# First attention of a transformer block: a third score buffer, values of two key tiles in one run, and the query projection over the whole array in blocks of seven passes

## The chip, the cores and the metric

The kernel runs on one core of one Trainium2 chip. A core has a matrix engine (TensorE, with a stationary operand that is loaded ahead of each multiplication), a vector engine (VectorE), an engine for functions such as exp (ScalarE), a general one (GpSimd), one that mainly issues transfers (SyncE), a working memory of 128 partitions (SBUF) and eight banks of accumulators that TensorE writes (PSUM, a bank holds 128 x 512 numbers of 4 bytes). The metric is the device time of one launch in microseconds (us), the median of several.

## The reference

One transformer block in float32: x is 2048 x 576, 32 heads of 18 numbers share one key head and one value head, and the second half is a feed-forward layer of two gates without a nonlinearity, 576 to 4608 and back.

```python
def A(x, wq, wk, wv, wo):
    q = (x @ wq).reshape(B, S, H, Dh) ...          # H = 32, Dh = 18
    k, v = x @ wk, x @ wv                          # one head for all
    p = softmax(einsum("bhqd,bkd->bhqk", q, k) * Dh ** -0.5)
    o = einsum("bhqk,bkd->bhqd", p, v)
    return o... @ wo
h = x + A(layernorm(x), ...)
n = layernorm(h)
out = h + ((n @ w_gate) * (n @ w_up)) @ w_down
```

## The kernel before, in words

The 2048 query rows are handled in four blocks of 512 (b = 0 to 3). Attention goes by groups of four heads (g = 0 to 7) and key tiles of 128 rows (t = 0 to 15); a tile has two *pairs* of heads (pr = 0 or 1), so a group has 32 pairs and a block 256. One pair is: two score matmuls (L701, 56 rows of the array each, one in the upper and one in the lower half, so that both run together) into a tile of two PSUM banks, and one exp on ScalarE over its 128 x 1024 numbers (L702), which writes a tile P in SBUF. The names are s{b}_{g}_{t}_{pr} and P{b}_{g}_{t}_{pr}. Two of the 56 rows carry an upper bound of the scores, which stands in for the maximum of the softmax.

*Values* of one key tile (L706) are four pairs of heads' products with V into four column groups of the accumulator `acc`: a run of eight matmuls in the records, in another tiling of the array (128 rows by 32 columns) than the scores (64 rows by 128 columns). `flush(n)` issues the values of the n oldest waiting tiles, in one piece. After the last tile of a group, VectorE transposes the accumulator (L732) and other steps (`run_aux`) normalise it.

Block 0 is the *first attention*. While its pairs run, the same code issues further work between them:

- `queries(b)`: the query projection of 512 rows by 126 columns (seven heads) per tile, 14 tiles in this stage. The product of two float32 matrices is made of 14 passes with a high and a low part of each side. Before, each pass is two matmuls, the upper and the lower 64 rows of the array, into two banks psq and psr (L498), which VectorE adds (L505 to L508); the result is stored to memory and fetched as the q of a group, together with the bounds.
- `bounds(b)`: sums of absolute values tq of the queries by head (L554, tile psg), split in a high and a low part by VectorE (L96, L97) and stored to `m_dram` by SyncE (L533). psg{b}_{n} begins at head n.
- `down_weights`: w_down is read, combined on GpSimd, split (L1500 on VectorE) and stored, one step for every two pairs.

The order on each engine is the order of the code (`manual_schedule`): nothing is rearranged. In `run` a loop issues pair, passes of the projection up to a budget (RATE = 2.3 of them per two pairs), pair, one auxiliary step, the values of all waiting tiles but the youngest. After the last tile of the projection (pair 208) the pools of the stage are closed and later ones are opened in the same memory, among them a second set of P tiles (P2, used in turn with the first six). After pair 226 stands the `guard`, a branch that is not taken with these inputs: it would compute exact maxima if the bound were too loose. All waiting values are issued ahead of it. Eight more pairs follow, then the other attentions mixed with the feed-forward layer, in all of which TensorE has work at every time.

PSUM before: two score tiles of two banks (tag s), two banks f, one bank m, one bank a. The accumulators of block 0 alternate between a and m up to group 5, the bound takes the one that is free:

```python
self.in_m = b == 0 and g < 6 and g % 2 == 1
return (self.ps_m if self.in_m else self.ps_a)(f"acc{b}_{g}")
```

The functions that the change touches, as they are before, with the line numbers of the profile:

## Time and profile before

| | |
|---|---|
| median of 3 runs | 2265.41 us (2263.82 to 2266.45) |
| the profiled execution | 2262.34 us, span from first to last instruction 2260.6 us |
| mean granted TensorE clock | 1.00 |
| up to pair 0 / pairs 0 to 226 / from the guard on | 43.6 / 253.9 / 1962.5 us |
| TensorE busy in the three | 31.6 / 250.7 / 1947.6 us |
| ScalarE busy in the three | 30.6 / 220.2 / 1175.8 us |
| values and scores in pairs 0 to 234 (L706, L701) | 124.4 us in 928 records, 106.1 us in 468 |
| half passes of the projection (L498) | 61.6 us in 196 records (psr) and 61.5 us in 196 (psq) |

Busy time is the union of an engine's instructions; matmuls are pipelined, so that the interval from one start to the next says more than the length of one. In rows of the timeline stand: start, length, engine, line, operation, tile written and tiles read, the part of the array that is used (rows * columns) or shapes, the count of instructions in the row, and in brackets the idle time before it on that engine and what ended it. In rows of groups "x" is the count, then come busy time, mean length in ns, and idle time before with its releaser. "PEld" is the loading of stationary operands.

### The profile page before, as it was taken

How to read it: one execution, taken by the hardware profiler on the slowest of the kernel's cores; microseconds unless marked ns; L12 is line 12 of the kernel's file. 1: busy time of each engine (PE TensorE's matmuls, PEld its weight loads, DVE VectorE, ACT ScalarE, POOL GpSimd, SP SyncE). 2: the span in 40 equal slices, each digit the busy share in tenths (PEclk: the TensorE clock that was granted, in tenths of full speed). 3: DMA queues.
4: the chain of work that ended last, by engine and by line, in shares of the span. 5: the costliest groups of instructions: out<-in, count | busy, mean ns of one | idle time of the engine just before them, and what ended most of it. 6: DMA issues, size and time to landing. Idle time of an engine off the chain costs nothing.

```text
span 2260.6 us, 45951 instructions
## 1 busy us (share of the span) xinstructions
PE 2229.9 (99%) x17972; PEld 1653.0 (73%) x17972; DVE 1381.2 (61%) x2234; ACT 1426.6 (63%) x1925; POOL 882.5 (39%) x956
## 2 busy tenths in 40 slices
PE   7999999999999999999999999999999999999999
PEld 5333345777778777777877777777777788999999
DVE  8565635555556557455555556555554667788776
ACT  7888877666666666666665666665666423555553
POOL 4445401444444444244444444433332344322222
PEclk9999999999999999999999999999999999999999
DMA  5879843555555555555455554654342435677775
GB/s 175 266 251 301 287 152 83 175 170 163 155 173 164 163 186 156 173 170 172 153 167 162 178 166 152 181 191 147 124 125 93 152 136 190 211 241 237 235 249 177
DMA packets 200433, 407.01 MB, mean 180 GB/s; under 512 B 22637, under 2 KB 54509, under 8 KB 200213
## 3 DMA queue, kind: packets, MB, share of 16 engines
q1 hardware_dynamic: 197621, 393.42, 54.4%
q0 software_dynamic: 2592, 10.62, 1.5%
q8 instruction: 143, 2.34, 0.4%
q14 instruction: 77, 0.63, 0.1%
HBM read 317.27 MB, written 74.55 MB: 173 GB/s over the span
## 4 chain that ended last, share of the span: by engine, by line
PE 81%; DMA 2%; POOL 1%; DVE 1%; ACT 1%; issue 1%; SPq 0%; ACTq 0%; POOLq 0%; DVEq 0%
PE pg L1073 17%; PE acc L706 15%; PE y L1023 12%; PE s L701 8%; PE gs L1297 8%; PE pu L1073 8%; PE yq L1262 4%; PE gu L1073 3%; PE yo L864 3%; PE gs L1304 2%; POOL h L1034 1%; PE y L993 1%; DMA out_dram<-h 1%; DMA wr<-in_wgu_dram 1%; DMA h<-in_x_dram 0%
## 5 line engine op out<-in xcount | busy, mean ns | idle before, releaser
L702 ACT ACTIVATE P<-s 128x1024 f32<-128x1024 f32 x1024 | 1009.8, 1028 | 218.8 <-PE s L701 138.3
L1073 PE MATMUL pg<-X,ws 64*128 64x512 f32 x2511 | 680.6, 389 | 0.9 <-DVE ob L719 0.9
L1073 PE MATMUL pu<-X,ws 64*128 64x512 f32 x2511 | 680.5, 389 | 0.2
L1073 PEld LDWEIGHTS pg<-X,ws 64*128 64x128 f32 x2511 | 465.0, 185 | 52.1 <-issue 2.7
L1073 PEld LDWEIGHTS pu<-X,ws 64*128 64x128 f32 x2511 | 464.2, 185 | 22.3 <-ACT tmp L1000 0.9
L706 PE MATMUL acc<-P,V 128*32 128x512 f32 x4096 | 479.9, 597 | 0.1
L701 PE MATMUL s<-q,kT 56*128 56x512 f32 x2048 | 431.4, 414 | 5.6 <-ACT P L702 4.5
L1034 POOL TENSOR_TENSOR h<-h,tmp 128x288 f32<-128x288 f32 x306 | 244.5, 829 | 335.8 <-ACT tmp L1033 333.5
L1033 ACT COPY tmp<-y 128x288 f32<-128x288 f32 x306 | 122.3, 400 | 356.0 <-PE y L1023 314.0
L701 PEld LDWEIGHTS s<-q,kT 56*128 56x128 f32 x2048 | 205.5, 184 | 166.8 <-ACT P L702 118.1
L1023 PEld LDWEIGHTS y<-wdo,room 128*128 128x128 f32 x2142 | 290.5, 188 | 47.3 <-issue 38.5
L1023 PE MATMUL y<-wdo,room 128*128 128x288 f32 x2142 | 306.8, 301 | 3.5 <-ACT tmp L1033 2.2
L706 PEld LDWEIGHTS acc<-P,V 128*32 128x32 f32 x4096 | 114.6, 109 | 254.9 <-issue 250.1
L951 DVE TENSOR_TENSOR ws<-wr,ws 128x1152 fp32r<-128x1152 f32 x108 | 189.9, 1759 | 100.0 <-POOL ws L948 100.0
L1029 DVE TENSOR_TENSOR h<-h,y 128x288 f32<-128x288 f32 x408 | 175.3, 452 | 118.0 <-PE y L1023 117.9
L1111 DVE TENSOR_TENSOR hf<-pu,hf 128x512 f32<-128x512 f32 x93 | 63.7, 685 | 223.7 <-ACT hf L1107 223.7
L948 POOL CAST ws<-wr 128x1152 fp32r<-128x1152 f32 x108 | 131.2, 1215 | 153.1 <-DMA wr<-in_wgu_dram 141.5
L96 POOL CAST room<-hf 128x256 fp32r<-128x256 f32 (+1 forms) x92 | 58.5, 636 | 319.9 <-DVE hf L1111 319.9
L1245 POOL TENSOR_TENSOR wsum<-wsum,wsum 128x512 f32<-128x512 f32 x72 | 145.2, 2017 | 45.4 <-DMA wsum<-in_wgs_dram 36.1
L97 DVE TENSOR_TENSOR room<-hf,room 128x256 fp32r<-128x256 f32 (+1 forms) x108 | 94.8, 878 | 3.3 <-ACT room L96 1.9
L1073 PE MATMUL gu<-X,ws 64*128 64x512 f32 x810 | 94.5, 389 | 0.0
L1073 PEld LDWEIGHTS gu<-X,ws 64*128 64x128 f32 x810 | 80.3, 184 | 11.9 <-issue 1.5
(268 smaller groups left out, 2759.1 us busy)
## 6 DMA issues: line engine op xcount, KB each, us to landing
wdo<-wd_dram SPq DMA_DIRECT2D x492, 288.0 KB
wr<-in_wgu_dram SPq DMA_DIRECT2D x108, 576.0 KB
wsum<-in_wgs_dram SPq DMA_DIRECT2D x108, 256.0 KB
wd_dram<-wd_room SPq DMA_DIRECT2D x20, 1008.0 KB
wsum_dram<-wsum SPq DMA_DIRECT2D x72, 256.0 KB
raw<-wsum_dram SPq DMA_DIRECT2D x72, 256.0 KB
q<-q_dram SPq DMA_DIRECT2D x64, 216.0 KB
raw<-in_wgs_dram SPq DMA_DIRECT2D x54, 256.0 KB
```

Of the source, the lines that this page charges most:

```text
L701: self.pe.matmul(s_[:, i], self.kT[o:o + 56, t * P:(t + 1) * P], q[o:o + 56, pr], start=True, stop=True)
L702: self.act.activation(p_, s_, AF.Exp, scale=SCALE)
L706: self.pe.matmul(acc[32 * j:32 * j + 32, :], self.V[:, t, :], Ps[j // 2][:, j % 2, :], start=first, stop=last, skip_group_check=True)
L948: self.nc.gpsimd.tensor_copy(w[:, 0], self.wr[n])
L951: self.dve.tensor_tensor(w[:, 1], self.wr.pop(n), f32(w[:, 0]), ALU.subtract)
L1023: pe.matmul(y[:, :HD], m[:, t * P:(t + 1) * P], k, start=(first and j == 0), stop=(j == 2), skip_group_check=True)
L1029: dve.tensor_tensor(hs, hs, y[:, :HD], ALU.add)
L1033: act.copy(z, y[:, :HD])
L1034: pool.tensor_tensor(hs, hs, z, ALU.add)
L1073: pe.matmul(ps, w[o:o + 64, wk, c], X[o:o + 64, xk, c], start=(j == 0), stop=(j == 26))
L1245: pool.tensor_tensor(to, x, y, op)
L1297: pe.matmul(bank[:, g * HT:(g + 1) * HT], W[:, wk, c, g], X[:, 2 * xk + c], start=(first and g == c == wk == xk == 0), stop=(c == 1 and wk ...
```

## The change

- **Third score buffer.** Within the first attention (from its first pair to the eighth pair behind the guard) the two banks f are given up for a third score tile of two banks, tag s3; `ps_s` counts its calls and gives every third one to s3. The bounds psg and the scores of the branch (again, psgl) also take a tile from `ps_s`. Four more P tiles (P1) are there as long as the projection runs.
- **Values of two key tiles in one run.** `twice` takes the place of `steps` and of the loop: four pairs with one `flush(2)` among them, behind the second pair if `even`, else behind the third; the auxiliary steps and those of `down_weights` stay at one for two pairs.
- **Projection.** A pass is one matmul over all 128 rows, into one bank (psq, now tag m). Seven passes are issued at a time, behind four pairs. VectorE only splits the sum (two operations less). RATE is now 0.56 blocks for each four pairs.
- The accumulators of block 0 are always in bank a.

```diff
     def ps_s(self, name):
+        self.n_s += 1
+        if self.pf is None and self.n_s % 3 == 0:
+            return self.p3.tile([P, 2, TB], F32, tag="s3", bufs=1, name=name)
         return self.ps.tile([P, 2, TB], F32, tag="s", bufs=2, name=name)
...
     def ps_acc(self, b, g):
-        self.in_m = b == 0 and g < 6 and g % 2 == 1
-        return (self.ps_m if self.in_m else self.ps_a)(f"acc{b}_{g}")
+        return self.ps_a(f"acc{b}_{g}")
...
-                psr = self.ps_f(f"psr{b}_{i}")
+                psq = self.ps_m(f"psq{b}_{i}")
                 for k, (w, m) in enumerate(passes(w_h, w_l, self.XT[b])):
-                    for o, ps in ((0, psq), (64, psr)):
-                        pe.matmul(ps[:r], w[o:o + 64], m[o:o + 64], start=(k == 0), stop=(k == 13))
-                    if k < 13:
+                    if k == 7:
                         yield 1
-                    if self.tqs and self.tqs[0][0] < max(b, 1) and (k == 12 or k >= 5 and 4 <= self.n_pair % (2 * NT) < 2 * NT - 6):
+                    if k in (0, 7) and self.tqs and self.tqs[0][0] < max(b, 1) and (k or 4 <= self.n_pair % (2 * NT) < 2 * NT - 6):
                         self.bounds(self.tqs[0][0])
+                    pe.matmul(psq[:r], w, m, start=(k == 0), stop=(k == 13))
                 qs = self.qb.tile([P, 2, TB], F32R, tag="qs", name=f"qs{b}_{i}")
-                t = f32(qs[:r, 0])
-                dve.tensor_copy(t, psr[:r])
-                dve.tensor_tensor(f32(qs[:r, 1]), psq[:r], t, ALU.add)
-                dve.tensor_copy(qs[:r, 0], f32(qs[:r, 1]))
-                dve.tensor_tensor(qs[:r, 1], f32(qs[:r, 1]), f32(qs[:r, 0]), ALU.subtract)
+                dve.tensor_copy(qs[:r, 0], psq[:r])
+                dve.tensor_tensor(qs[:r, 1], psq[:r], f32(qs[:r, 0]), ALU.subtract)
...
-            psg = (self.ps_a if self.in_m else self.ps_m)(f"psg{b}_{self.known[b]}")
+            psg = self.ps_s(f"psg{b}_{self.known[b]}")[:, 0]
...
+    def twice(self, even, work=iter(())):
+        for i in range(4):
+            if i == (2 if even else 3):
+                self.flush(2)
+                self.run_aux(1)
+                next(work, None)
+            self.pair()
+        self.run_aux(1)
+        next(work, None)
...
-                    while live:
-                        self.pair()
-                        due += RATE
-                        while due > 0 and live:
-                            z = next(others, None)
-                            live = z is not None
-                            due -= z or 0
-                        self.pair()
-                        self.run_aux(1)
-                        self.flush(len(self.pend) - 1)
-                        next(work, None)
+                    with tc.tile_pool(name="P1", bufs=P1_BUFS) as self.p1:
+                        self.pair()
+                        self.pair()
+                        live = True
+                        while live:
+                            due += RATE
+                            self.twice(due >= 1, work)
+                            if due >= 1:
+                                due -= 1
+                                live = next(others, None) is not None
...
-            self.steps(lambda: self.n_pair < n, work)
+            while self.n_pair < n:
+                self.twice(True, work)
...
-            self.steps(lambda: self.n_pair < n + 8)
+            while self.n_pair < n + 8:
+                self.twice(True)
+            two.close()
+            self.p3, self.pf = None, pool("f", 1, space=PSUM)
...
-RATE = 2.3
+RATE = 0.56
+P1_BUFS = 4
```

In the following rows the first index of a name (block 0) is left out, s_0_10_0 is s0_0_10_0, and the last number is that of the buffer.

TensorE in the middle of the stage, group 0; before, tiles 9 to 11:

```order
L701 MATMUL s_0_9_1_864<-q_0_421,kT 128x512 x2
L706 MATMUL acc_0_640<-P_0_8_0_832,V 32x512 x2
L706 MATMUL acc_0_640<-P_0_8_1_850,V 32x512 x2
L701 MATMUL s_0_10_0_877<-q_0_421,kT 128x512 x2
L498 MATMUL psq_3_882<-XT_94,wq_0_676 126x512
L498 MATMUL psr_3_883<-XT_94,wq_0_676 126x512
L498 MATMUL psq_3_882<-XT_94,wq_0_676 126x512
L498 MATMUL psr_3_883<-XT_94,wq_0_676 126x512
L701 MATMUL s_0_10_1_888<-q_0_421,kT 128x512 x2
L706 MATMUL acc_0_640<-P_0_9_0_860,V 32x512 x2
L706 MATMUL acc_0_640<-P_0_9_1_865,V 32x512 x2
```

The same place of the changed kernel, from the bound psg_7 to the run behind the block:

```order
L698 MATMUL s_0_7_1_791<-q_0_424,kT 128x512 x2
L551 MATMUL psg_7_799<-tq_1_677,G 32x512
L503 MATMUL psq_2_798<-XT_94,wq_0_569 126x512 x2
L503 MATMUL psq_2_798<-XT_94,wq_1_570 126x512
L503 MATMUL psq_2_798<-XT_94,wq_0_569 126x512 x2
L503 MATMUL psq_2_798<-XT_94,wq_1_570 126x512
L503 MATMUL psq_2_798<-XT_94,wq_0_569 126x512
L698 MATMUL s_0_8_0_813<-q_0_424,kT 128x512 x2
L698 MATMUL s_0_8_1_818<-q_0_424,kT 128x512 x2
L698 MATMUL s_0_9_0_828<-q_0_424,kT 128x512 x2
L703 MATMUL acc_0_643<-P_0_6_0_767,V 32x512 x2
L703 MATMUL acc_0_643<-P_0_6_1_772,V 32x512 x2
```

The passes of the projection have moved out from between two pairs into a block behind four of them, three pairs stand between a block or a run and the next run, a run has the values of two tiles (its third and fourth row, of P_0_7_0 and P_0_7_1, follow), and the bound lies directly ahead of a block. In the program as built, the banks that psg7 took are not given out again before s_0_11_1; meanwhile s_0_8_1 and s_0_9_0 lie in one and the same two banks, and so do s_0_10_0 and s_0_10_1. The same happens around psg21: s_1_6_1 and s_1_7_0, s_1_8_0 and s_1_8_1 share banks, up to s_1_10_0. Around the other bounds no two neighbours share. In the whole stage there are 28 blocks, 27 of them between pair 16 and pair 208.

ScalarE where the stage's pools have been closed, group 6; before, with the engines' counters (PE, Activation, DVE, Pool) and those of the transfers (DMAHW) that each waits for:

```order
L702 ACTIVATE P_6_14_0_3132<-s_6_14_0_3131 128x1024 [waits PE_49,Activation_49]
L702 ACTIVATE P_6_14_1_3137<-s_6_14_1_3136 128x1024 [waits PE_49,Activation_49]
L702 ACTIVATE P_6_15_0_3152<-s_6_15_0_3151 128x1024 [waits DMAHW3_49,DMAHW2_49,DMAHW4_49,DMAHW1_49,DMAHW5_49,DMAHW0_49,DMAHW6_49,DVE_49,DMAHW7_49,PE_49,Pool_49]
L702 ACTIVATE P_6_15_1_3157<-s_6_15_1_3156 128x1024 [waits PE_49]
L702 ACTIVATE P_7_0_0_3172<-s_7_0_0_3171 128x1024 [waits PE_49]
```

And in the changed kernel:

```order
L699 ACTIVATE P_6_11_0_2839<-s_6_11_0_2838 128x1024 [waits PE_49,Activation_49]
L699 ACTIVATE P_6_11_1_2844<-s_6_11_1_2843 128x1024 [waits PE_49,Activation_49]
L699 ACTIVATE P_6_12_0_2873<-s_6_12_0_2872 128x1024 [waits DMAHW2_49,DMAHW3_49,DMAHW1_49,DMAHW4_49,DMAHW0_49,DMAHW5_49,DVE_49,DMAHW6_49,PE_49,DMAHW7_49,Activation_49,Pool_49]
L699 ACTIVATE P_6_12_1_2878<-s_6_12_1_2877 128x1024 [waits PE_49]
L699 ACTIVATE P_6_13_0_2891<-s_6_13_0_2890 128x1024 [waits PE_49]
```

The first tile of the pool P2, which waits for everything that used the memory before, has moved from P_6_15_0 to P_6_12_0, the first pair behind the last bounds (psg3_0).

TensorE behind the guard; before:

```order
L701 MATMUL s_7_1_0_9662<-q_7_2888,kT 128x512 x2
L701 MATMUL s_7_1_1_9667<-q_7_2888,kT 128x512 x2
L706 MATMUL acc_7_9672<-P_7_0_0_3172,V 32x512 x2
L706 MATMUL acc_7_9672<-P_7_0_1_3177,V 32x512 x2
L701 MATMUL s_7_2_0_9677<-q_7_2888,kT 128x512 x2
L701 MATMUL s_7_2_1_9682<-q_7_2888,kT 128x512 x2
L706 MATMUL acc_7_9672<-P_7_1_0_9663,V 32x512 x2
L706 MATMUL acc_7_9672<-P_7_1_1_9668,V 32x512 x2
```

And in the changed kernel:

```order
L698 MATMUL s_7_1_0_9434<-q_7_2680,kT 128x512 x2
L698 MATMUL s_7_1_1_9439<-q_7_2680,kT 128x512 x2
L703 MATMUL acc_7_9444<-P_7_0_0_2945,V 32x512 x2
L703 MATMUL acc_7_9444<-P_7_0_1_2950,V 32x512 x2
L703 MATMUL acc_7_9444<-P_7_1_0_9435,V 32x512 x2
L703 MATMUL acc_7_9444<-P_7_1_1_9440,V 32x512 x2
L698 MATMUL s_7_2_0_9453<-q_7_2680,kT 128x512 x2
L698 MATMUL s_7_2_1_9458<-q_7_2680,kT 128x512 x2
```

Before, each run of values there belongs to a tile older than the last one; now the run's second tile is the one whose scores stand directly ahead of it.

## The prediction, made before the changed kernel ran

> **What bounds the stage now.** I read the page first, then the timeline of the first attention, the groups and waits of ScalarE there, then rows at single places.

> ```profile
> span 2260.6 us, 45951 instructions
> PE   7999999999999999999999999999999999999999
> ACT  7888877666666666666665666665666423555553
> PEclk9999999999999999999999999999999999999999
> 43.60:64.70 21.10, 6.92 (x32) 2.84 (x32) 1.00 0.66 204
> 64.70:276.10 211.40, 87.45 (x384) 36.15 (x384) 1.00 0.83 276
> 276.10:297.50 21.40, 8.07 (x36) 3.29 (x37) 1.00 0.63 210
> 297.50:304.60 7.10, 3.66 (x16) 1.49 (x16) 1.00 0.90 313
> L702 ACT ACTIVATE P<-s 128x1024 f32<-128x1024 f32 x193 | 187.3, 1024 | 24.9 <-PE s L701 24.9
> L701 PE MATMUL s<-q,kT 56*128 56x512 f32 x384 | 87.5, 452 | 0.8 <-ACT P L702 0.8
> ```

> TensorE is full everywhere at a clock of 1.00, ScalarE is at 0.8 or so in the first attention. The four window rows count the score matmuls (two to a pair), so they give the stage by pairs: pairs 0 to 16 in 21.1 us, 16 to 208 in 211.4 (1.10 a pair, 2.20 a step of two), 208 to 226 in 21.4, the next eight in 7.1 and a little more. The last two rows are of the second window: ScalarE waits 24.9 us for scores, TensorE 0.8 for ScalarE. The stage is bound by TensorE's order, ScalarE has 12% to spare. What a step costs TensorE:

> ```profile
> 163.09 0.49 PE L701 MATMUL s<-q,kT 56*128 56x512 f32 x2
> 163.43 0.39 PE L498 MATMUL psq<-XT,wq 64*126 64x512 f32 x1
> 163.66 0.39 PE L498 MATMUL psq<-XT,wq 64*126 64x512 f32 x1
> 163.69 1.94 ACT L702 ACTIVATE P<-s 128x1024 f32<-128x1024 f32 x2 [0.18 <-PE s L701]
> 163.89 0.39 PE L701 MATMUL s<-q,kT 56*128 56x512 f32 x2
> 164.21 1.07 PE L706 MATMUL acc<-P,V 128*32 128x512 f32 x8
> 165.21 0.50 PE L701 MATMUL s<-q,kT 56*128 56x512 f32 x2
> 165.81 3.84 ACT L702 ACTIVATE P<-s 128x1024 f32<-128x1024 f32 x4 [0.18 <-PE s L701]
> 167.80 0.18 PEld L701 LDWEIGHTS s<-q,kT 56*128 56x128 f32 x2 [0.17 <-ACT P L702]
> ```

> From start to start: the first pair after a run of values 0.34 (163.09 to 163.43), a pass or pair within one mode of the array 0.23, the last before another mode 0.32, a run of one key tile 1.00. So two 0.10s belong to each change of mode. ScalarE: first exponential 0.60 after its scores start, then one every 0.92 (1.94 less 1.02; four in 3.84 make 0.94). A bank is free about 1.05 after its exponential starts: the scores at 167.80 waited for the second of the four, started at 166.75.

> **Part 1, values of two key tiles in one run.** One such run exists in the trace:

> ```profile
> 325.36 1.92 PE L706 MATMUL acc<-P,V 128*32 128x512 f32 x16
> 327.21 0.74 PE L701 MATMUL s<-q,kT 56*128 56x512 f32 x4
> ```

> 1.85 against twice 1.00, and one change of mode less (0.20): 0.35 saved for each merged pair of runs.

> **Part 2, projection in blocks of seven over the whole array.** Whole-array passes stand in the trace before the stage:

> ```profile
> 38.67 1.78 PE L482 MATMUL psq<-XT,wq 128*126 128x512 f32 x7
> 40.28 1.09 PE L264 MATMUL psk<-XT,w_h 128*128 128x512 f32 x4
> 43.31 0.39 PE L264 MATMUL psk<-XT,w_l 128*128 128x512 f32 x1
> 43.63 0.72 PE L701 MATMUL s<-q,kT 56*128 56x512 f32 x4
> L264 PEld LDWEIGHTS psk<-XT,w_h x36: 186/188/268, 14.3 to 42.9; 128*128 128x128 f32 x36
> ```

> Seven take 1.61 (38.67 to 40.28), 0.23 each: no less than a pair of half passes, so 196 passes save nothing. But half passes share the scores' mode and whole ones do not: 43.31 to 43.63 is again 0.32 before a change. A block costs 7 x 0.23 + 4 x 0.10 = 2.02, and 0.40 of it is new, 28 times. [...]

> **Part 3, the third buffer, over pairs 16 to 208.** The last bounds of the stage, used here and in part 5:

> ```profile
> 284.60 1.11 PE L554 MATMUL psg<-tq,G 126*32 126x512 f32 x4
> 285.64 0.50 PE L701 MATMUL s<-q,kT 56*128 56x512 f32 x2
> 285.75 0.68 DVE L96 CAST m<-psg 32x512 fp32r<-32x512 f32 x1 [4.33 <-PE psg L554]
> 286.46 0.68 DVE L97 TENSOR_TENSOR m<-psg,m 32x512 fp32r<-32x512 f32 x1
> 287.17 0.34 SPq L533 DMA_DIRECT2D m_dram<-m  x1
> ```

> In the order a round of four pairs is followed by a block (call it Q) or not (N); mostly N and Q alternate. From the first score after a block, at 0: scores 0, 0.34, 0.57, run at 0.90, score 2.75, 3.09, third one when its bank is free (exponential begun at 2.44, free 3.49), run 3.92, scores 5.77 and 6.11, block 6.43, next score about 8.3. So N and Q take 8.33 for eight pairs, where TensorE alone needs 2.98 + 5.01. A Q behind a Q takes 5.01. The order has 27 blocks and 48 rounds between pair 16 and pair 208: 21 x 8.33 + 6 x 5.01 = 205.0. To that come two single bound matmuls of 0.35 and two sets of four at 1.05 (284.60 to 285.64): 207.8 against 211.4. This is the gain of the change, 3.6.

> **Part 4, bounds in a score buffer.** After psg7 and psg21 the bank of the bound is not given out again for seven and eight pairs, and twice each time two neighbouring pairs get the same bank (s_0_8_1 and s_0_9_0, s_0_10_0 and s_0_10_1, and again in group 1). The second must wait for the first's exponential. From s_0_8_0 at 0: exponentials 0.60, 1.52; s_0_9_0 at 2.57; run 3.0; scores 4.86, 5.20, the next same-bank one at 7.45; run 7.9; scores 9.7, 10.1, block 10.4, s_0_12_0 at 12.3. Eight pairs in 12.3, not 8.33: 3.9 more, twice, 7.8. The floor is 2.2 each (4.3 of lost ScalarE time less the slack of one cycle, 1.0, and less what the next round's slack gives back).

> **Part 5, the stage's ends.** Pairs 0 to 16: five passes fewer (-1.2), two runs merged (-0.7), one block's changes (+0.4), and ScalarE is close, so between -1.5 and 0; I take -0.7. Pairs 208 to 226: without blocks ScalarE sets the pace with 18 x 0.92 = 16.6, plus the 2.6 of idle around the guard that stays, plus the wait for these stores and loads:

> ```profile
> wd_room<-in_wd_dram POOLq DMA_DIRECT2D x10, 576.0 KB, 5.4
> m_dram<-m SPq DMA_DIRECT2D x3, 112.0 KB
> ```

> The first exponential in the memory of the freed pools (P_6_15_0 before, P_6_12_0 now) waits for all DMAs from there. Before, the store of the last bounds lay some six pairs back; now it is the very next pair. The store is issued 2.57 after psg (284.60 to 287.17); ScalarE, with two scores in hand, would go on 1.75 after it. Landing takes at least the 0.34 of its issue and at most the 5.4 of a load five times its size; I take 2.0, near the small end by its size: ScalarE is held 2.8, bounds 1.2 and 6.2. A run of 1.85 behind drained banks costs 1.2 once more. 16.6 + 2.6 + 2.8 + 1.2 = 23.2, of which about 0.6 overlap: 22.6 against 21.4, +1.2. The eight pairs after the guard: nothing is pending there, so each run of two tiles stands right behind its own last pair. ScalarE's work ends 0.9 after the last exponential begins; the run can only end about 1.0 after that one is free, and the next score needs 0.60: ScalarE stands 1.7 in each of two rounds, 3.4, where it now loses 0.6. +2.8.

> **What costs nothing.** The cover is read from VectorE's rows:

> ```profile
> 155.38 0.72 DVE L732 STREAM_TRANSPOSE os<-acc 128x512 f32<-128x512 f32 x1 [4.21 <-PE acc L706]
> 162.70 1.32 DVE L1500 TENSOR_TENSOR wd_room<-wd_room 128x1152 f32<-128x1152 f32 x1
> 165.98 0.69 DVE L505 COPY qs<-psr 126x512 f32<-126x512 f32 x1 [1.97 <-PE psr L498]
> ```

> VectorE's two operations less for each of 14 tiles: it waited 1.97 us for the passes anyway (165.98). The four further P buffers and SyncE's stores moved by a block: queries are fetched a group ahead. The down weights' work on GpSimd, its queue and SyncE's keeps one step for two pairs.

> One cover gets thin: with all accumulators in bank a the transpose (0.72) must end before the next group's first run. Three scores lie between, 0.9 on TensorE, 2.8 at ScalarE's pace; behind a 1.32 operation it would be late by up to 1.2. I count 0, and keep it as a rival.

> **Sum.** -0.7 - 3.6 + 7.8 + 1.2 + 2.8 = +7.5 us. After the stage the code is the same and TensorE full, so it stays to the end. The profiled execution took 2262.34 (span 2260.6), so 2269.8 for it; it lies 3 below the median of the runs, 2265.41, which makes 2272.9. From no change a measurement of this kernel tells about 0.2%, 4.5 us.

> **Rivals.**
> - The late banks cost nothing beyond ScalarE's slack (part 4 falls away). For it: ScalarE has 24.9 us of waits to give. Against: they lie in other rounds. -0.3: 2265. It decides from the point where one same-bank wait costs under 1.2 instead of 1.95. Chance 0.13.
> - Changes of mode into and out of a block are hidden, since three buffers keep ScalarE fed. 28 x 0.40 off: 2261.7, not slower. Against it stand 43.31 to 43.63 and 163.09 to 163.43. [...] Chance 0.08, half of it faster by over 0.2%.
> - The single accumulator bank: six group changes at up to 1.2, 2280. The 4.21 of idle before the transpose speaks against it. Chance 0.06.
> - Weight loads of whole passes do not overlap: 2272.9 + 196 x 0.188 = 2310. The 1.78 row is against it. Chance 0.02.
> - The forecast: 0.71, one part in eight of it under +4.5.

> So faster 0.04, same 0.04 + 0.13 + 0.09 = 0.26, slower 0.70. Range: the forecast's own lower ends (-1.5, -3.6, 2.2 for each late bank, 0.3, 1.5) give +1 and the upper ones (0, -3.6, 7.8, 5, 3) +12, so 2266.5 to 2278; to leave out no more than 2 in 10 it takes in the first rival: 2264.5 to 2278.

> **What will show it.** Runs x16 of 1.85 in the stage; blocks of 1.71 with 0.34 behind; a pair of rounds of 8.3 us late in the stage and of about 12 after psg7 and psg21; TensorE waiting for ScalarE about 1.9 at s_0_9_0; P_6_12_0 waiting for a DMA 2 to 3 us; ScalarE idle twice 1.7 after the guard. I am wrong if the stage from pair 16 to 208 is not within 3 us of 215, if weight loads show in the blocks, or if later stages change their length.

## The result, and the profile after

The changed kernel took 2283.48 us in the median of four runs (2277.57 to 2289.25), the kernel before 2264.61: a ratio of 1.0083 with a 95% interval of 1.0056 to 1.0110. Forecast were 2272.9 and a range to 2278: slower, as said, but by 18.9 us instead of 7.5. The profiled execution is the shortest of the four, 2277.57 (span 2275.8) against 2262.34.

The row of the core (span, mean granted clock), then two groups of the page (busy time, mean ns, idle time before):

```profile
core 0: 2275.8 us, clock 0.996
```

```profile
L703 PE MATMUL acc<-P,V 128*32 128x512 f32 x4096 | 476.2, 601 | 2.8 <-DVE os L729 2.7
L698 PE MATMUL s<-q,kT 56*128 56x512 f32 x2048 | 411.2, 413 | 15.8 <-ACT P L699 13.5
```

Two things are new. TensorE waits 15.8 us for scores (5.6 before) and 2.8 for accumulators (0.1), and the granted clock is not 1.00. The score matmuls by stage, as shown for the kernel before (length, TensorE's busy time, weight loads, granted clock, DMA share, GB/s):

```profile
43.70:63.80 20.10, 6.67 (x32) 2.64 (x32) 1.00 0.66 197
63.80:285.10 221.30, 71.68 (x384) 30.68 (x384) 0.98 0.80 268
285.10:309.50 24.40, 7.54 (x37) 3.02 (x37) 0.93 0.69 241
```

| | before | after | difference | forecast |
|---|---|---|---|---|
| pairs 0 to 16 | 21.1 | 20.1 | -1.0 | -0.7 |
| pairs 16 to 208 | 211.4 | 221.3 | +9.9 | -3.6 + 7.8 = +4.2 |
| pairs 208 to 226 | 21.4 | 24.4 | +3.0 | +1.2 |
| the eight behind the guard | 8.0 | 9.5 | +1.5 | +2.8 |
| all the rest | | | +1.8 | 0 |

```profile
63.98:67.39 3.41, 1.58 (x14) 0.59 (x18) 1.77 (x3) 2.42 (x3) 1.75 (x3) 1.00 0.50 140
67.39:70.81 3.42, 3.42 (x20) 0.72 (x8) 2.41 (x3) 0.69 (x2) 0.99 (x2) 0.50 0.68 239
70.81:74.22 3.41, 1.75 (x16) 0.60 (x18) 0.00 (x0) 2.81 (x3) 3.41 (x5) 1.00 0.94 333
104.94:108.35 3.41, 1.55 (x14) 0.60 (x18) 0.00 (x0) 2.75 (x3) 0.00 (x0) 1.00 1.05 374
108.35:111.77 3.42, 3.42 (x14) 1.29 (x7) 0.00 (x0) 1.21 (x3) 0.57 (x1) 0.50 0.28 65
162.97:166.38 3.41, 0.68 (x6) 0.34 (x10) 3.32 (x6) 2.73 (x3) 0.00 (x0) 1.00 0.85 273
166.38:169.79 3.41, 3.41 (x18) 0.57 (x10) 1.82 (x3) 0.00 (x0) 3.28 (x5) 0.50 1.09 385
296.09:299.50 3.41, 1.55 (x9) 0.63 (x7) 0.32 (x2) 3.10 (x4) 0.00 (x0) 1.00 0.00 0
299.50:302.91 3.41, 3.41 (x18) 0.59 (x16) 0.00 (x0) 2.51 (x3) 0.00 (x0) 0.50 0.43 90
1876.46:1879.87 3.41, 1.23 (x10) 1.22 (x10) 0.65 (x3) 0.80 (x2) 3.16 (x8) 1.00 0.71 231
1879.87:1883.29 3.42, 3.42 (x16) 2.86 (x17) 2.36 (x6) 1.29 (x3) 2.08 (x3) 0.50 1.04 398
```

TensorE was busy 1.58, 1.55, 0.68, 1.55 and 1.23 us of a cell, and each time the whole next cell ran at half clock; with 1.75 (70.81) it did not (1.00 from 74.22 to 77.63). A cell at half clock is called halved here. Five halved cells lose up to 1.7 us each, 8.5 together. The other 6.7 of the 15.2 are the waits less what the change gains, close to the 7.5 forecast. In pairs 16 to 208 the difference of 9.9 is made of three parts: TensorE idles 10.9 us instead of 1.8 (9.1 more), loses 5.1 to the three halved cells, and its own work is 4.3 shorter. The idle time of a cell need not be one wait. At 296 us it was three:

```profile
297.48 0.50 PE L698 MATMUL s<-q,kT 56*128 56x512 f32 x2 [1.15 <-ACT P L699]
298.39 0.49 PE L698 MATMUL s<-q,kT 56*128 56x512 f32 x2 [0.30 <-ACT P L699]
299.31 0.65 PE L698 MATMUL s<-q,kT 56*128 56x512 f32 x2 [0.42 <-ACT P L699]
```

The last place (1876) is in the kernel before as well, an idle time of 2.2 us between two stages. The only change of the clock in the span of its profiled execution is at the end, at 2260.49; counted back from there in steps of 3.4133 us, 1.75 us of that idle time lie in the cell at 1861:

```profile
1861.13:1864.54 3.41, 1.66 (x13) 1.42 (x11) 1.76 (x3) 0.83 (x3) 3.00 (x8) 1.00 0.24 49
1864.54:1867.96 3.42, 3.00 (x21) 2.73 (x23) 1.93 (x5) 1.66 (x4) 3.42 (x5) 1.00 1.01 346
2260.49:2260.55 0.06, 0.00 (x0) 0.00 (x0) 0.00 (x0) 0.00 (x0) 0.00 (x0) 0.51 0.00 0
```

TensorE was still busy 1.66 us of it, just under half, and the next cell ran at 1.00.

### The profile page after: what moved, and what is told of

Its sections match the earlier page's. It is cut to its first block, busy times and chain, and to the rows that moved or that the text cites. A ratio compares the mean times of both kernels' runs of the same rounds, so it can differ in the third digit from the quotient of the medians.

```text
span 2275.8 us, 45521 instructions
## 1 busy us (share of the span) xinstructions
PE 2233.7 (98%) x17776; PEld 1645.7 (72%) x17776; DVE 1361.1 (60%) x2206; ACT 1421.8 (62%) x1925; POOL 878.3 (39%) x956
## 4 chain that ended last, share of the span: by engine, by line
PE 83%; POOL 1%; ACT 1%; DVE 1%; DMA 0%; issue 0%; SPq 0%; ACTq 0%; POOLq 0%; DVEq 0%
PE pg L1070 21%; PE acc L703 15%; PE y L1020 12%; PE s L698 9%; PE gs L1294 8%; PE yq L1259 4%; PE pu L1070 4%; PE gu L1070 4%; PE yo L861 3%; PE gs L1301 1%; POOL h L1031 1%; PE y L990 1%; ACT P L699 0%; PE tx L917 0%; ACT tmp L1030 0%
## 5 line engine op out<-in xcount | busy, mean ns | idle before, releaser
L698 PE MATMUL s<-q,kT 56*128 56x512 f32 x2048 | 411.2, 413 | 15.8 <-ACT P L699 13.5
L703 PEld LDWEIGHTS acc<-P,V 128*32 128x32 f32 x4096 | 121.4, 110 | 274.9 <-issue 262.0
L698 PEld LDWEIGHTS s<-q,kT 56*128 56x128 f32 x2048 | 196.2, 185 | 150.4 <-ACT P L699 65.8
## 6 DMA issues: line engine op xcount, KB each, us to landing
wr<-in_wgu_dram SPq DMA_DIRECT2D x108, 576.0 KB
```

The source lines that it names most:

```text
L698: self.pe.matmul(s_[:, i], self.kT[o:o + 56, t * P:(t + 1) * P], q[o:o + 56, pr], start=True, stop=True)
L703: self.pe.matmul(acc[32 * j:32 * j + 32, :], self.V[:, t, :], Ps[j // 2][:, j % 2, :], start=first, stop=last, skip_group_check=True)
```

## The experiments

Theory A: the change costs waits of TensorE, and on top halved cells behind them. Theory B: the waits alone. Theory C: the blocks over the whole array, with their changes of mode, are what costs.

**The four late banks.** Bounds go to bank m between two tiles of the projection, so no neighbours share banks:

```diff
-            psg = self.ps_s(f"psg{b}_{self.known[b]}")[:, 0]
+            psg = self.ps_m(f"psg{b}_{self.known[b]}")
...
                             if due >= 1:
...
+                            elif self.tqs and not self.open and self.tqs[0][0] < NB - 1 and (self.tqs[0][0] == 0 or len(self.tqs) == 4):
+                                self.bounds(self.tqs[0][0])
```

> The changed kernel, but each bound of the queries goes to bank m between two tiles of the projection, in a round without a block, so that no two neighbouring score tiles share their banks any more (four such places before). Theory A (two parts: waits of TensorE, and, behind each stretch of 3.41 us in which it is less than half busy, 3.41 us at half clock, about 1.7 us each): the late banks' waits go, 7.8 us by the prediction's arithmetic, and with them the halved stretches there (two of the four of the stage in the profiled execution): some 7.8 + 3 us less than the changed kernel, about 2272 to 2274. Theory B (only waits count, the clock is incidental): 7.8 less, about 2276, with halved stretches still there or not. Theory C (the blocks over the whole array and their mode changes are what costs): no change, 2283.

Measured 2272.21 (ratio to the kernel before 1.0040, its interval 1.0027 to 1.0053), within A's 2272 to 2274. But against the median of all eight executions of the changed kernel (2281.5, with the repetition below) it is 9 less, between A's 11 and B's 8, so this run does not separate the two; C is out. In its trace no cell near the four places is halved, and pairs 16 to 208 take 208.2 us, where part 3 of the prediction had 207.8 without late banks. A new wait came in its place, on VectorE and then TensorE:

```profile
65.27 0.68 DVE L98 CAST m<-psg 32x512 fp32r<-32x512 f32 x1 [3.11 <-DMA q_dram<-qs]
66.81 1.40 PE L504 MATMUL psq<-XT,wq 128*126 128x512 f32 x5 [3.25 <-DVE m L99]
```

The bound's halves share two SBUF buffers with the query tiles, whose store had not landed; the next block needs bank m and stands 3.25 us.

**The ends.** The P tiles restart at the old six, and single tiles follow the guard:

```diff
             self.wp, self.hh, self.p2 = pool("w", 2), pool("hid", 4), pool("P2", P2_BUFS)
+            self.p_next = -1
...
-            while self.n_pair < n + 8:
-                self.twice(True)
+            self.steps(lambda: self.n_pair < n + 8)
```

> The changed kernel, but the P tiles start again at the first of the old six when the stage's pools are closed, so that the first exponential in new memory comes some six pairs later, and behind the guard values go one tile at a time again. Theory A: 1.8 and 3.4 us of waits go by the prediction's arithmetic, and the halved stretch behind the guard with them (1.7 where it occurs): 5 to 7 less than the changed kernel, about 2277. Theory B: 5 less, 2278. Theory C: no change, 2283.

Measured 2280.39 (1.0081, 1.0065 to 1.0096), 1 to 3 less than the changed kernel: the 5 are not resolved in the time. In its trace the wait of 2.9 us on ScalarE is gone, no cell there is halved, and pairs 208 to 234 take 29.1 us, against 33.8 and 32.2 in the two traces of the changed kernel, although TensorE stood longer at the guard's branch (last section).

**The transpose.** VectorE's splits and the down weights' steps are held while a group's last tile is pending:

```diff
                 self.flush(2)
+                for f in self.late:            # splits of a projection tile that ended meanwhile
+                    f()
+                self.late = []
                 self.run_aux(1)
-                next(work, None)
+                self.tick(work)                # owes a step while a pending tile has t == NT - 1
```

> The changed kernel, but while the last tile of a group waits for its values, VectorE's splits of the projection and the down weights' steps are held back until the group's transpose has been issued. Theory A: the wait of 2.7 us for the transpose at the fourth group and the halved stretch behind it go: 4 to 5 less, about 2279. Theory B: 2.7 less, 2281. If the transpose is not what is waited for (rival), no change.

Measured 2284.36 (1.0095, 1.0081 to 1.0110): no gain. No accumulator waited for a transpose in its trace, but at 180 us a score tile waited 3.19 us for VectorE's split of a bound whose banks it takes over, and a halved cell followed. The lateness had moved; its cause is in VectorE's queue, below.

**The same kernel again.**

> The changed kernel once more, for other positions of the 3.41 us grid against the program. Theory A: the same waits at the same places, but halved stretches at other ones of the six places that can fall under half busy, and a time that differs by about 1.7 us for each of them; no halved stretch without such a place ahead of it. Theory B: time does not go with the number of halved stretches.

Measured 2279.65 (2273.11 to 2284.03; 1.0068, 1.0050 to 1.0085). In its trace the cells caught were other ones of the same places, so the grid lay elsewhere against the program: both waits behind psg7, one behind psg21, the transpose (two cells), the one at 1881, and an early one at 55 us. Ahead of the early one TensorE was busy 2.43 us of the cell, so A does not account for it. Over the eight executions of the changed kernel the span goes from 2271.3 at a mean clock of 0.998 to 2287.5 at 0.992. A straight line through them gives 0.56 us for each us at half clock (standard error 0.06, so that the 0.5 of a clock at half is not excluded), and 2265.8 at none (standard error 1.6); 42 executions of the kernel before give 2260.3 at none. So some 5.5 us are the waits less the gains, and the rest, some 12 us in the mean, is the clock.

**Late banks on purpose, empty and filled.** In a kernel with the bounds in m and the edited ends (the first of the last three below) a score tile is held ten times for eight pairs; the second kernel fills the waits:

```diff
+        if self.n_pair in HOLDS:                       # 38, 54, ... 182
+            self.held = self.ps.tile([P, 2, TB], F32, tag="s", bufs=2, name=f"held{self.n_pair}")
+            self.busy(1)
+        if self.n_pair - 8 in HOLDS:
+            self.busy(1)
+            self.held = None
+        if self.held is not None and self.n_s % 3 == 1:
+            self.busy(FILL)                            # pairs of score matmuls into held: 0, or 4
```

> The kernel with bounds in bank m and edited ends, and late banks put back on purpose, in number: ten times a score tile is held for eight pairs and written by one pair of matmuls at its start and one at its end, so that 28 times two neighbouring score tiles share their banks and TensorE stands for about 1.9 us each time. Waits alone (theory B): 28 times 1.3 (a part is given back by slack), some 36 us more than the kernel without, about 2300. Theory A adds a halved stretch for about every second of them (those that lie well inside one cell of the 3.41 us grid), 10 to 15 at 1.7 us: 2315 to 2325.

> The same 28 late banks, but ahead of each second tile four more pairs of score matmuls (0.23 us each, result not used) run into the held tile while TensorE would stand: the waits stay, TensorE is busy in them, and it has 0.9 us more to do each time, of which some does not fit into the wait. Waits and work alone (theory B): 10 us more than the kernel with the late banks unfilled, about 2310. Theory A: few halved stretches or none, so 2308 to 2314 and faster than the unfilled one, although it does more.

Measured 2304.04 (1.0170, 1.0155 to 1.0186) and 2313.78 (1.0219, 1.0204 to 1.0235). A's expectation missed: the filled one is slower, and the clock is 0.995 and 0.997. The waits were the reason: nearly all of the added ones were 0.9 to 1.2 us, not 1.9, and left their cells over half busy. The three idle times of 1.86 were each followed by a halved cell. As a test of A it is inconclusive; it shows that waits of up to 1.2 us, one to a cell, cost no clock there.

**The late banks of the changed kernel, filled.**

```diff
+        if self.n_pair in (18, 21, 46, 49):    # ahead of the late score tile
+            self.busy(5)                       # score matmuls into the bound's tile, second bank
+        if self.n_pair in (22, 51):
+            self.busy(1)
```

> The changed kernel with its four late banks as they are, but ahead of the second score tile of each such pair five more score matmuls (0.22 us each, their result not used) run into the unused second bank of the bound's tile, while TensorE would stand; one more keeps that tile until it was given back before. The waits stay (1.8 us at each place, by 0.5 us in all more to do). Theory A: no halved stretch behind these four places, which by their lengths (1.7 to 1.9 us of 3.41) give some 2 of them in an execution: 3 us faster than the changed kernel although it does more, about 2278 where the eight runs of the changed one have a median near 2281. Theory B: 0.5 us slower, and as many halved stretches.

Measured 2285.84 (1.0105, 1.0090 to 1.0120): not faster. The four places had TensorE busy 2.1 to 2.9 us of their cells, and none was followed by a halved one; but the fill waited for VectorE's read of the tile (1.33 us at one place), and five other cells were halved, one behind a new wait of 2.64 us at 242. Inconclusive as to time.

**Idle times of two lengths.** So the question was put where nothing else is short: the kernel before, 36 pairs of the later attentions, between matmuls of the feed-forward layer.

```diff
+        if b > 0 and 0 < g < 7 and t in (5, 10) and pr:
+            for _ in range(n):                         # 0, or 1
+                self.act.activation(p_, s_, AF.Exp, scale=SCALE)
+            for j in range(4):
+                self.pe.matmul(s_[32 * j:32 * j + 32, 0], self.V[:, 0, :], p_[:, j % 2, :], ...)
```

> The kernel before, with 36 short stands of TensorE put into the later stages, where it is the bound and everything else has slack: behind the scores of 36 chosen pairs four more value matmuls read that pair's exponential and write over the score tile (not used), so that TensorE stands until the exponential is ready, about 1.4 us (0.60 to its start, 1.02 for it, less 0.23 for the scores). Each place costs that, the added run of 0.25 and two changes of mode, about 1.9 us: 68 us in all, 2331. Theory A and B agree here if a stand of 1.4 us leaves each cell of 3.41 us more than half busy: no halved stretches beyond the one of the kernel before.

> The same 36 places, but the exponential is computed twice in a row, so that TensorE stands for about 2.4 us each time. Theory B (a stand costs its length): 1.0 us more for each place than with the short one, 104 us in all, 2367. Theory A (a cell of the 3.41 us grid in which TensorE is less than half busy is followed by one at half clock): a stand of 2.4 us covers half of one cell in some 0.7 of all positions, so about 25 halved stretches at 1.7 us on top, 42 us: 2409, with a granted clock near 0.98.

Measured 2356.79 (1.0409, 1.0379 to 1.0439) and 2441.81 (1.0785, 1.0753 to 1.0816). The added matmuls as a group, and the core, with the exponential once:

```profile
L698 PE MATMUL s<-P,V 128*32 128x512 f32 x288 | 39.2, 617 | 46.9 <-ACT P L711 46.9
```

```profile
core 0: 2355.6 us, clock 0.998
```

And with the exponential twice:

```profile
L698 PE MATMUL s<-P,V 128*32 128x512 f32 x288 | 51.3, 790 | 83.8 <-ACT P L696 83.8
```

```profile
core 0: 2439.0 us, clock 0.977
```

The idle time before them is 46.9 us (1.1 to 1.63 us at 35 places, and 3.62 at one, where ScalarE had another tile to convert first) and 83.8 (2.2 to 2.7, and 3.59 at that same place). The one long place of the shorter kernel:

```profile
983.47 1.93 PE L698 MATMUL s<-P,V 128*32 128x512 f32 x8 [3.62 <-ACT P L711]
```

The only two halved cells of that kernel (982.07 to 988.90) stand there; none follows any of its other 35 places. In the longer one 30 of the 36 places are followed by a halved cell; at the six others the edge of two cells lies in the idle time, and neither cell holds more than 1.80 us of it. The longer one adds 36.9 us of idle time, but 83.4 to the span: 46.5 more, with 32 halved cells instead of 2, so 1.55 us for a cell. B (2367, or 36 more than the shorter one) is excluded; A's step of 78 is near the 85 measured. The short ones had been priced at 1.9 a place and cost 2.5. One cell with the longer idle time and the one behind it:

```profile
604.47:607.88 3.41, 0.72 (x10) 0.20 (x10) 2.01 (x4) 3.08 (x4) 0.65 (x2) 1.00 0.85 268
607.88:611.29 3.41, 3.41 (x18) 1.58 (x12) 2.75 (x2) 0.00 (x0) 1.78 (x3) 0.50 0.48 160
```

And with the shorter one, 1.63 us in one cell, which stays over half busy:

```profile
589.54:592.95 3.41, 1.78 (x20) 1.21 (x20) 3.19 (x6) 3.19 (x4) 1.35 (x2) 1.00 0.83 211
592.95:596.37 3.42, 3.42 (x30) 2.13 (x32) 1.64 (x1) 1.02 (x1) 2.13 (x2) 1.00 0.77 240
```

Over fourteen traces (the changed kernel and all experiments, from 45 us on), 74 cells had TensorE busy for less than half, and 70 of them were followed by a halved one; of some 9,100 others 25 were, nine of these halved themselves and ten at about 50 us, where the stage begins. What decides those ten stays open. The half is of busy time by the records, in which a matmul that takes 0.23 from start to start stands with 0.39.

**Without the third buffer.** All scores go to the two tiles of tag s, in the last kernel of this section.

```diff
-        if self.pf is None and self.n_s % 3 == 0:
+        if self.n_s < 0:
```

> The same kernel without the third score tile: all scores go to the two of tag s, the runs of two tiles and the blocks stay. Part 3 of the prediction says that the third tile pays for the longer runs: without it each run of 1.85 us and each block of 2.0 leaves ScalarE with too little in hand; by the same arithmetic as there, TensorE stands about 1 us more for every four pairs, 226 / 4 x 1 to be lost, some 50 us: about 2315. If the third tile were not needed, no difference.

Measured 2311.62 (1.0212, 1.0196 to 1.0227), 46 more than with it. TensorE's score matmuls in the stage without it:

```profile
L700 PE MATMUL s<-q,kT 56*128 56x512 f32 x404 | 79.8, 454 | 40.1 <-ACT P L701 40.1
```

And with it:

```profile
L700 PE MATMUL s<-q,kT 56*128 56x512 f32 x385 | 70.8, 443 | 0.6
```

The first row covers some ten pairs more. In pairs 16 to 208 alone the stage takes 251.0 us without the tile and 210.0 with it, and 38.2 us of the 251.0 are waits for ScalarE, in pieces of 0.95 in the mean: long runs and blocks need the third tile, and pieces of that length cost hardly any clock (0.997).

**Toward a version without the waits.** Three kernels with bounds in m and both edits at the ends: as they are; with an SBUF tile of their own for the bounds' halves and the down weights' steps held while one of a group's last two tiles is pending; and with that tile but no hold. The tile, and the hold:

```diff
-            m2 = self.qb.tile([H, 2, TB], F32R, tag="qs", name=f"m2_{b}_{lo}")
+            m2 = self.qb.tile([H, 2, TB], F32R, tag="m2", bufs=1, name=f"m2_{b}_{lo}")
...
-                next(work, None)
+                self.tick(work)                # owes a step while a pending tile has t >= NT - 2
...
-P1_BUFS = 4
+P1_BUFS = 3
```

> The changed kernel with bounds in bank m and with both edits at the ends, without the hold of the down weights' steps and with the bounds' halves in the tag of the query tiles. Theory A: what the bounds alone gave (2272.2) less the 5 us of waits and the halved stretch at the ends: about 2265; the difference to the kernel with all edits is the wait for the first bound's store (3.3 us) and for the transposes (0 to 3), and the halved stretches that they cause.

> Everything that the first runs pointed to in one kernel: bounds in bank m between two tiles of the projection (their halves in an SBUF tile of their own, since the first of them waited 3.2 us for the store of a query tile; three further P tiles instead of four), no steps of the down weights while one of a group's last two tiles waits for its values, P tiles that start again at the old six, single tiles behind the guard. The gain of the three buffers and the merged runs stays (3.6 us by the prediction, and 1 to 2 from fewer waits at the ends), and no place of the stage should lie under half busy. Theory A: 2258 to 2262, faster than the kernel before (2264.2), with at most one halved stretch in the stage. If the blocks themselves cost more than the trace of before showed (theory C): 2265 or more.

> The kernel with bounds in bank m and edited ends, with an SBUF tile of their own for the bounds' halves and three further P tiles, and no hold of the down weights' steps (which moved VectorE's late work in front of a query split, 4.85 us). The 4.8 us wait for the store and the two halved stretches behind it go: 2272.1 less 4.8 and 1.7 to 3.4, about 2265, with some wait for VectorE's queue (1 to 3 us) left. If the wait for VectorE only moves on to another place, 2270.

Measured 2272.14 (1.0028, 1.0019 to 1.0037), 2272.91 (1.0032, 1.0020 to 1.0044) and 2265.68 (1.0011, 1.0002 to 1.0020). The first missed its 2265 by 7 and the second its 2262 by 11; the third came out as expected. With the hold, VectorE at group 2:

```profile
125.02 1.97 DVE L1519 TENSOR_TENSOR wd_src<-wd_src,wd_hi 128x864 f32<-128x864 f32 x1 [6.78 <-POOL wd_hi L1513]
128.52 1.32 DVE L1519 TENSOR_TENSOR wd_src<-wd_src,wd_hi 128x1152 f32<-128x1152 f32 x1
129.76 0.68 DVE L506 CAST qs<-psq 126x512 fp32r<-126x512 f32 x1
131.22 1.22 PE L504 MATMUL psq<-XT,wq 128*126 128x512 f32 x2 [4.85 <-DVE qs L507]
```

The first row waits 6.78 us for GpSimd, and the query's split stands behind it; the next block needs the one bank that this split frees. The third kernel is some 16 us better than the changed one and level with the kernel before, not faster: in its trace pairs 16 to 208 take 210.0 us (211.4 before), a wait of 2.2 and a halved cell among them, and from there to the eighth pair behind the guard it takes 4.2 more than the kernel before. In the traces of all three kernels the branch at the guard took 4.7 to 5.7 us instead of 0.4 (last section), with a halved cell behind it, which no expectation had. In the third kernel TensorE stood 4.40 us there, 4.0 more than before, and with the 1.7 of the halved cell that is more than the 4.2. Whether the third kernel would be faster without that is not shown.

## Why the prediction was right and wrong

- **The waits and most of their sizes: right.** TensorE at the late banks behind psg7 in the changed kernel, then ScalarE at the stage's ends:

```profile
63.80 0.73 PE L698 MATMUL s<-q,kT 56*128 56x512 f32 x4
66.36 0.50 PE L698 MATMUL s<-q,kT 56*128 56x512 f32 x2 [1.83 <-ACT P L699]
72.65 0.50 PE L698 MATMUL s<-q,kT 56*128 56x512 f32 x2 [1.66 <-ACT P L699]
296.40 5.61 ACT L699 ACTIVATE P<-s 128x1024 f32<-128x1024 f32 x6 [2.91 <-PE s L698]
313.60 3.77 ACT L699 ACTIVATE P<-s 128x1024 f32<-128x1024 f32 x4 [1.58 <-PE s L698]
318.96 2.86 ACT L699 ACTIVATE P<-s 128x1024 f32<-128x1024 f32 x3 [1.58 <-PE s L698]
```

  s_0_9_0 comes 2.56 after s_0_8_0 (2.57 forecast), and the eight pairs from there on take 13.6 us, those behind psg21 13.8: some 11.9 and 12.1 without the halved cell in each (12.3 forecast). P_6_12_0 was held 2.91 (2.8 forecast). Its row names TensorE, but those scores had ended at 293.16; the store of the last bounds was issued at 294.17, and the hold went when the edit of the ends moved the tile. ScalarE idled 1.58 twice behind the guard (1.7), yet the eight pairs there took 1.5 more and not 2.8, so that term was too large. The rival "late banks cost nothing" is out by the first experiment.
- **Blocks, runs, third buffer: right.** From the same kernel:

```profile
178.04 0.97 PE L698 MATMUL s<-q,kT 56*128 56x512 f32 x6
178.94 1.92 PE L703 MATMUL acc<-P,V 128*32 128x512 f32 x16
180.79 1.26 PE L698 MATMUL s<-q,kT 56*128 56x512 f32 x6
184.50 1.88 PE L503 MATMUL psq<-XT,wq 128*126 128x512 f32 x7
186.31 0.97 PE L698 MATMUL s<-q,kT 56*128 56x512 f32 x6
```

  A run is 1.85 (178.94 to 180.79), a block with its exit 1.81, eight pairs 8.27 (178.04 to 186.31; 8.33 forecast). The weight loads of the blocks (0.188 in the mean) lie under the passes: seven of both in a row would make 7 x (0.23 + 0.188) = 2.9, not 1.81. Of these 1.81, 0.20 are more than seven times 0.23, so the changes of mode are paid: two rivals fall. The shorter work of 4.3 us in pairs 16 to 208 is near the 3.6 forecast.
- **The single accumulator bank: mis-sized.** The prediction counted 0 from one row with 4.21 us of idle time before the transpose, with 1.2 as the rival's price. Measured is 2.70, once in six group changes:

```profile
160.37 3.23 DVE L1508 TENSOR_TENSOR wd_src<-wd_src,wd_hi 128x864 f32<-128x864 f32 x2 [14.25 <-POOL wd_hi L1502]
163.52 0.68 DVE L505 CAST qs<-psq 126x512 fp32r<-126x512 f32 x1
165.44 0.71 DVE L729 STREAM_TRANSPOSE os<-acc 128x512 f32<-128x512 f32 x1
166.20 3.52 PE L703 MATMUL acc<-P,V 128*32 128x512 f32 x16 [2.70 <-DVE os L729]
```

  VectorE had been idle 14.25 us, not for lack of work but because the head of its queue waited for GpSimd; everything behind it came late together. That the alternating accumulators had absorbed this before is argued; putting a second one back was not tried, since no bank is free.
- **The sum: a term was missing.** It added TensorE's idle times at their own length, and "TensorE full, so it stays to the end" was taken to settle the rest. The clock at 1.00 was read in the first rows, and the prediction did not ask what holds it there. Each cell with some 1.8 us or more of idle time, in one piece or several, could cost another 1.55 to 1.7 in these runs. By the fit the waits less the gains are 5.5 us (7.5 forecast) and the clock, which the sum put at nothing, some 12. The prediction's own sign of being wrong came true: pairs 16 to 208 took 221.3, not within 3 of 215. Of the 5.7 above its 215.6, 5.1 are the three halved cells; the 2.70 of the transpose was largely made up by the late banks and the shorter work, which came out somewhat better than forecast.

The position of the grid differs between executions: counted back in steps of 3.4133 us, its first edge lies some 0.9 us behind the start of the span in the kernel before, 2.5 in the changed one and 0.3 in the kernel with the longer idle times. That fits the 16 us over which the changed kernel's times spread. An idle time of 1.74 us (in the repetition) to 1.86 us was enough where one cell held it, while 1.66 us was not, nor 1.75 in the kernel before, nor 1.77 to 1.80 in three cells of the kernel with the longer idle times, so that the border is not sharp by these records.

## What to carry to other kernels

Where TensorE is full, price idle times by their length only as long as no cell of 3.41 us holds more than some 1.6 us of them (1.63 and 1.66 had no halved cell behind them here); from 1.8 us on, in one piece or several (1.83 and 1.86 had one), add the chance that a cell falls under half busy, times the 1.55 to 1.7 us that a halved cell cost in these runs. Read idle time in front of an instruction as slack only after asking what the head of that queue waits for. Before a second bank of a buffer is given away, list every engine's queue whose lateness that bank absorbed.

## What was not expected of the hardware

The branch at the guard, whose body is skipped, took TensorE 0.39 to 0.48 us in seven of fifteen traced executions, the kernel before and the changed one among them, and 1.6 to 5.7 in the other eight. Of the seven kernels with the edits at the ends six had a long one, of the other eight executions two (1.7 both). The first scores behind it in the last kernel that was meant to be faster:

```profile
300.03 1.11 PE L700 MATMUL s<-q,kT 56*128 56x512 f32 x4 [4.40 <-PEq L579]
```

Why the lengths differ no run shows; it stays open.
